# An order of its own for ScalarE during attention: sigmoids, roundings and weight conversions in source order

## The chip, the core and the metric

The kernel runs on one core of a Trainium2 chip. TensorE (PE, with its weight loads as PEld), VectorE (DVE), ScalarE (ACT), GpSimd (POOL) and SyncE (SP) work side by side and are held together by semaphores. The metric is the device time of one execution in microseconds (us). Three executions of the kernel before took 722.46 to 725.92 us, with a median of 723.36 us.

## The reference

The computation is a chain of three layers, all in float32.

```python
scores = scale * q @ k.T - log(S)            # batch 4, 12 heads, S = 448, head_dim 64
x = (1 / (1 + exp(-scores))) @ v             # sigmoid attention, -> (1792, 768)
h = max(x @ w1, x @ w2, x @ w3) @ w_out      # max of three products
h = h @ w_in                                 # (1792, 1024)
solu = h * softmax(h); ln = layernorm(solu) * g_ln
out = ln @ w_out2                            # (1792, 768)
```

The weights arrive as 64-bit floats (their two 32-bit words are in the input), so the core makes float32 values of them itself.

## The kernel before

**Precision.** A large product is computed as three TensorE products of rounded parts: every operand is split into a rounded high part (`copy`, L48) and the rest (`rest`, L54), and high times high, high times low and low times high are added in PSUM.

**Attention** (the loop from L317) goes over 24 pairs of heads, `pr` from 0 to 23. For each pair, `prep_qk` (L222) splits k and q on VectorE into `kt` and `qt`; `scores(pr, c)` (L266), for four chunks c of 128 rows (448 rows and 64 of padding), issues six matmuls into a PSUM tile `sc` and one sigmoid on ScalarE (L281) that writes `sf`. There are three `sc` tiles, so the fourth chunk of a pair waits until the pair's first sigmoid has emptied its tile. `attend(pr, c)` (L286) multiplies `sf` by v into a PSUM tile `av`. After a pair's fourth chunk, ScalarE rounds `av` to `xh` (L50 by way of L303) and VectorE writes the rest `xl` (L55 by way of L304). In each turn TensorE does the four scores of pair pr, the last two `attend` of pair pr - 1, and the first two `attend` of pair pr. k and q are loaded two pairs ahead by SyncE's DMA queue into two buffers, v into three.

**Weights.** In the background runs a queue of generators. `prepare(key)` (L163) turns one 128 x 768 piece of weights into float32 and splits it: a scaling on ScalarE (L147, out `y_...`, called a conversion here), then on VectorE a shift (L150), a shift with OR (L153), a rounding (L52) and a rest (L55). The 64-bit words of a piece (768 KB) lie in one of two buffers `raw`. Once L153 has read one, `load_next` (L132) issues the load of the next piece from GpSimd's DMA queue. Each `run_bg(n)` in the source takes n steps of the queue; a piece has five steps (scaling, shift, shift with OR, rounding, rest). The eleven pieces of `first` (L114: eight of `wi`, three of `wo`) are the ones that are queued during attention.

**After attention** `gen_w` (L242) multiplies w_out by w_in once (tiles `pw`), and then follow the products with the three weights (`pg`, L356) and with the combined weights (`h`, L428), the layer norm, and the last product (`po`, L503).

**What sets the order.** The source is traced into instructions, and a scheduler puts each engine's instructions into a fixed order by readiness and priorities of its own. Each engine then executes its row strictly from first to last. L68 exempts TensorE: `tc.manual_schedule` keeps its instructions in the order of the source. ScalarE, VectorE and the DMA queues are ordered by the scheduler; it may pull an instruction ahead of others that stand earlier in the source.

Of the kernel before, what the change touches and what calls it, by code (L numbers as in the profile page):

```python
# [33 lines left out]
def sigmoid_attention_max_moe_solu_ln(tc, q, k, v, w123, wo, wi, w2, g, out):  # L34
# [13 lines left out]
    def copy(eng, dst, src):  # L48
        if eng is act:
            act.copy(dst, src)  # L50
        else:
            eng.tensor_copy(dst, src)  # L52

    def rest(eng, dst, src, hi):  # L54
        eng.tensor_tensor(out=dst, in0=src, in1=hi.bitcast(F32), op=ALU.subtract)  # L55
# [8 lines left out]
    def shut(*cms):  # L64
        for cm in cms:
            cm.__exit__(None, None, None)
# [30 lines left out]
    def run_bg(n=1):  # L97
        while n > 0 and bg:
            if next(bg[0], "end") == "end":
                bg.popleft()  # L100
            else:
                n -= 1
# [29 lines left out]
    def load_next():  # L132
        i = state["load"]
        if i >= len(stream):
            return
        state["load"] += 1
        key = stream[i]
        t = rawp.tile([P, U, 2], I32, tag="raw", name=f"raw{i}", bufs=RAWS)
        pool.dma_start(out=t, in_=source(key).rearrange("p (n t) -> p n t", t=2))
        raws[key] = t  # L140
# [74 lines left out]
    def load_v(pr):  # L215
        if pr >= NP:
            return
        vr = apool.tile([P, 2, 4, D], F32, tag="vr", name=f"vr{pr}", bufs=3)
        sp.dma_start(out=vr, in_=v[pr])
        v_ops[pr] = vr  # L220

    def prep_qk(pr):  # L222
        if pr >= NP:
            return
        qr, kr = qk_raw.pop(pr)
        kt = apool.tile([P, 2, SX], F32R, tag="kt", name=f"kt{pr}")
        qt = apool.tile([P, 2, S], F32R, tag="qt", name=f"qt{pr}")
        qk_ops[pr] = (qt, kt)
        copy(dve, kt[:, 0], kr)
        copy(dve, qt[:, 0], qr)  # L230
        rest(dve, kt[:, 1], kr, kt[:, 0])
        rest(dve, qt[:, 1], qr, qt[:, 0])
        load_qk(pr + 2)
# [32 lines left out]
    def scores(pr, c):  # L266
        qt, kt = qk_ops[pr]
        sc = ps_sc.tile([P, 2, 512], F32, tag="sc", name=f"sc{pr}_{c}")
        terms = ((0, 0), (0, 1), (1, 0))
        for t, (x, y) in enumerate(terms):  # L270
            for j in range(2):
                rows = slice(j * D, (j + 1) * D)
                pe.matmul(  # L273
                    sc[:, j, :S],
                    lhsT=kt[rows, x, c * P : (c + 1) * P],
                    rhs=qt[rows, y],
                    start=(t == 0),
                    stop=(t == len(terms) - 1),
                )
        sf = apool.tile([P, 2, S], F32, tag="sf", name=f"sf{pr}_{c}", bufs=6)  # L280
        act.activation(sf, sc[:, :, :S], AF.Sigmoid, bias=bias_s, scale=1.0 / math.sqrt(D))  # L281
        weights[(pr, c)] = sf
# [3 lines left out]
    def attend(pr, c):  # L286

        b, hp = divmod(pr, NPAIR)
        vr = v_ops[pr]
        if c == 0:  # L290
            pas[pr] = ps_av.tile([P, 512], F32, tag="av", name=f"av{pr}")
        pa = pas[pr]
        sf = weights.pop((pr, c))
        for j in range(2):
            pe.matmul(pa[j * D : (j + 1) * D, :S], lhsT=vr[:, j, c], rhs=sf[:, j], start=(c == 0), stop=(c == 3))  # L295
        if c < 3:
            return
        pas.pop(pr)
        v_ops.pop(pr)
        if hp == 0:  # L300
            xs_hi[b] = xps[b].tile([P, KC, S], F32R, name=f"xh{b}")
            xs_lo[b] = xps[b].tile([P, KC, S], F32R, name=f"xl{b}")
        copy(act, xs_hi[b][:, hp], pa[:, :S])  # L303
        rest(dve, xs_lo[b][:, hp], pa[:, :S], xs_hi[b][:, hp])  # L304
        load_v(pr + 3)


    act.preload_act_table_set("sigmoid_and_others")
    for pr in range(2):
        load_qk(pr)  # L310
# [6 lines left out]
    for pr in range(NP):  # L317
        if pr == 1:
            load_next()
            load_next()  # L320
        for c in range(4):
            scores(pr, c)
            if c == 1:
                prep_qk(pr + 1)
        if pr > 1:
            run_bg(1)
        if pr > 0:
            attend(pr - 1, 2)
            attend(pr - 1, 3)
        if pr > 1:  # L330
            run_bg(1)
        attend(pr, 0)
        attend(pr, 1)
        if pr > 1:
            run_bg(1)
    attend(NP - 1, 2)
    attend(NP - 1, 3)
    run_bg(1 << 20)
    for cm, _ in reversed(ps1):
        shut(cm)  # L340
# [245 lines left out]
```

## Time and profile before

| | |
|---|---|
| median of three executions | 723.36 us (722.46 to 725.92) |
| the profiled execution | 724.43 us, of which the span is 722.7 us |
| PE busy | 698.5 us (97%) |
| DVE busy | 334.0 us (46%) |
| ACT busy | 237.7 us (33%) |
| chain that ended last | PE 93%, DMA 3% |

The span runs from the first to the last instruction of the profile; 1.73 us of the execution lie around it. A busy PE isn't PE at its peak, since matmuls overlap; so the pace of attention is read from the distance between the starts of one pair and the next. The granted clock is 1.00 at TensorE's full 2.4 GHz and 0.50 at 1.2 GHz; values between are means over a stretch in which it changed.

### The profile page before, as it was taken

How to read it: one execution, taken by the hardware profiler on the slowest of the kernel's cores; microseconds unless marked ns; L12 is line 12 of the kernel's file. 1: busy time of each engine (PE TensorE's matmuls, PEld its weight loads, DVE VectorE, ACT ScalarE, POOL GpSimd, SP SyncE). 2: the span in 40 equal slices, each digit the busy share in tenths (PEclk: the TensorE clock that was granted, in tenths of full speed). 3: DMA queues.
4: the chain of work that ended last, by engine and by line, in shares of the span. 5: the costliest groups of instructions: out<-in, count | busy, mean ns of one | idle time of the engine just before them, and what ended most of it. 6: DMA issues, size and time to landing. Idle time of an engine off the chain costs nothing.

```text
span 722.7 us, 9080 instructions
## 1 busy us (share of the span) xinstructions
PE 698.5 (97%) x3664; PEld 576.0 (80%) x3664; DVE 334.0 (46%) x610; ACT 237.7 (33%) x396; POOL 32.6 (5%) x59
## 2 busy tenths in 40 slices
PE   6777999999999999999999999999999999999997
PEld 3334555556888999999999999988999999999997
DVE  4897444431552354435433322215755555555440
ACT  5576666663222033132310200202322332322221
POOL 1111000000221000000000000000000000000000
PEclk9899999999999999999999999999999999999999
DMA  7777544420564124232331000800322222222221
GB/s 261 264 259 258 170 127 126 127 72 13 203 221 175 44 88 132 92 127 88 111 107 44 1 0 1 349 0 1 110 93 97 81 81 80 81 81 81 89 94 44
DMA packets 29707, 80.82 MB, mean 112 GB/s; under 512 B 3424, under 2 KB 12896, under 8 KB 28896
## 3 DMA queue, kind: packets, MB, share of 16 engines
q1 hardware_dynamic: 22176, 42.48, 17.1%
q0 software_dynamic: 7488, 37.75, 15.0%
q8 instruction: 29, 0.48, 0.3%
q14 instruction: 14, 0.11, 0.1%
HBM read 62.13 MB, written 18.09 MB: 111 GB/s over the span
## 4 chain that ended last, share of the span: by engine, by line
PE 93%; DMA 3%; DVE 1%; issue 1%; ACT 1%; SPq 0%; ACTq 0%
PE pg L239 36%; PE po L512 16%; PE h L436 16%; PE av L295 10%; PE sc L273 8%; PE pw L239 7%; DMA kr<-in_k 1%; ACT sf L281 1%; DMA raw<-in_wo 1%; DMA raw<-in_wi 1%; DVE y_wi L153 0%; PE pt L496 0%; DVE qt L55 0%; DVE y_wi L150 0%; DVE kt L55 0%
## 5 line engine op out<-in xcount | busy, mean ns | idle before, releaser
L239 PE MATMUL pg<-xh,r_w 128*128 128x448 f32 x864 | 245.5, 365 | 0.0
L239 PEld LDWEIGHTS pg<-xh,r_w 128*128 128x128 f32 x864 | 162.3, 188 | 12.9
L239 PE MATMUL pg<-xl,r_w 128*128 128x448 f32 x432 | 157.8, 365 | 0.0
L436 PE MATMUL h<-wf,hh 128*128 128x512 f32 x336 | 103.8, 390 | 0.8 <-issue 0.8
L281 ACT ACTIVATE sf<-sc,bias_s 128x896 f32<-128x896 f32 x96 | 88.9, 1006 | 31.4 <-PE sc L273 31.4
L273 PE MATMUL sc<-qt,kt 64*128 64x448 f32 x576 | 73.8, 392 | 19.7 <-ACT sf L281 14.4
L273 PEld LDWEIGHTS sc<-qt,kt 64*128 64x128 f32 x576 | 52.4, 191 | 47.9 <-ACT sf L281 22.9
L239 PEld LDWEIGHTS pg<-xl,r_w 128*128 128x128 f32 x432 | 81.1, 188 | 6.4
L295 PE MATMUL av<-sf,vr 128*64 128x448 f32 x384 | 82.4, 574 | 0.0
L374 DVE TENSOR_TENSOR h<-pg,h 128x448 f32<-128x448 f32 x48 | 29.9, 623 | 101.9 <-PE pg L239 101.9
L512 PE MATMUL po<-w2h,lh 128*128 128x384 f32 x224 | 75.0, 335 | 0.0
L512 PE MATMUL po<-w2h,ll 128*128 128x384 f32 x224 | 75.0, 335 | 0.0
L512 PE MATMUL po<-w2l,lh 128*128 128x384 f32 x224 | 74.9, 334 | 0.0
L436 PEld LDWEIGHTS h<-wf,hh 128*128 128x128 f32 x336 | 62.8, 188 | 13.6 <-issue 1.1
L436 PE MATMUL h<-wf,hl 128*128 128x512 f32 x168 | 65.6, 390 | 0.0
L295 PEld LDWEIGHTS av<-sf,vr 128*64 128x64 f32 x384 | 26.8, 144 | 44.8 <-issue 38.3
L448 DVE TENSOR_REDUCE st<-h 128x1 f32<-128x1024 f32 x14 | 17.1, 1222 | 84.9 <-PE h L436 84.9
L147 ACT ACTIVATE y_w<-raw 128x768 f32<-128x768 f32 x26 | 23.3, 897 | 100.3 <-DVE r_w L55 93.2
L50 ACT CAST hh<-h 128x128 fp32r<-128x128 f32 x84 | 18.1, 295 | 93.3 <-PE h L436 86.5
L239 PE MATMUL pw<-wih,r_wo 128*128 128x512 f32 x144 | 44.6, 390 | 0.0
L372 ACT COPY h<-pg 128x448 f32<-128x448 f32 x24 | 12.8, 533 | 92.3 <-PE pg L239 92.3
L512 PEld LDWEIGHTS po<-w2h,lh 128*128 128x128 f32 x224 | 42.1, 188 | 0.5
(68 smaller groups left out, 626.1 us busy)
## 6 DMA issues: line engine op xcount, KB each, us to landing
raw<-in_w POOLq DMA_DIRECT2D x26, 768.0 KB, 4.6
kr<-in_k SPq DMA_DIRECT2D x24, 256.0 KB, 2.8
raw<-in_wi POOLq DMA_DIRECT2D x8, 768.0 KB, 4.8
vr<-in_v SPq DMA_DIRECT2D x24, 256.0 KB, 3.7
w_d<-ws POOLq DMA_DIRECT2D x12, 512.0 KB, 3.7
wf<-w_d SPq DMA_DIRECT2D x6, 1024.0 KB, 9.9
u_d<-ub SPq DMA_DIRECT2D x12, 512.0 KB, 2.9
ut<-u_d SPq DMA_DIRECT2D x48, 128.0 KB, 3.1
```

What stands on the lines that cost most here:

```text
L50: act.copy(dst, src)
L147: act.activation(y, raw.bitcast(F32)[:, :, 1], AF.Prelu, scale=2.0**-112, alpha=2.0**32)
L239: pe.matmul(ps, lhsT=l, rhs=r, start=(i == 0), stop=(i == n - 1))
L273: pe.matmul(sc[:, j, :S], lhsT=kt[rows, x, c * P : (c + 1) * P], rhs=qt[rows, y], start=(t == 0), stop=(t == len(terms) - 1),)
L281: act.activation(sf, sc[:, :, :S], AF.Sigmoid, bias=bias_s, scale=1.0 / math.sqrt(D))
L295: pe.matmul(pa[j * D : (j + 1) * D, :S], lhsT=vr[:, j, c], rhs=sf[:, j], start=(c == 0), stop=(c == 3))
L372: act.copy(hv, ps[:, :S])
L374: dve.tensor_tensor(out=hv, in0=ps[:, :S], in1=hv, op=ALU.max)
L436: pe.matmul(ps[:, n], lhsT=l, rhs=r, start=(f == 0 and i == 0), stop=(f == FC - 1 and i == 2))
L448: dve.tensor_reduce(out=nmax, in_=ps, axis=AX.XY, op=ALU.max, negate=True)
L512: pe.matmul(ps[:, :hw], lhsT=l, rhs=r, start=(kc == 0 and i == 0), stop=(kc == K2 - 1 and i == 2))
```

## The change

The source of the attention loop gets a second `manual_schedule`, for ScalarE, from the table load to the end of the loop. Within it ScalarE issues in source order. The three `run_bg(1)` of a pair, which stood between the scores and the `attend` calls from pair 2 on, become one `run_bg(3)` at the end of the turn, from pair 3 on. Three steps of five mean that at most one scaling falls into a turn. VectorE, GpSimd and SyncE are ordered by the scheduler as before.

```diff
+    first_order = tc.manual_schedule(engines={mybir.EngineType.Activation})
+    first_order.__enter__()
     act.preload_act_table_set("sigmoid_and_others")
...
             scores(pr, c)
             if c == 1:
                 prep_qk(pr + 1)
-        if pr > 1:
-            run_bg(1)
         if pr > 0:
             attend(pr - 1, 2)
             attend(pr - 1, 3)
-        if pr > 1:
-            run_bg(1)
         attend(pr, 0)
         attend(pr, 1)
-        if pr > 1:
-            run_bg(1)
+        if pr > 2:
+            run_bg(3)
     attend(NP - 1, 2)
     attend(NP - 1, 3)
+    shut(first_order)
     run_bg(1 << 20)
```

TensorE's and GpSimd's instructions stand in the same order before and after. ScalarE's row at the start of attention, before (`sf1_2` is the sigmoid of pair 1, chunk 2; `y_wi_0_1` the scaling of the second piece of `wi`; the last number of a name is a serial number):

```order
L147 ACTIVATE y_wi_0_0_304<-raw0_193 128x768
L281 ACTIVATE sf0_0_149<-sc0_0_142,bias_s_94 128x896
L281 ACTIVATE sf0_1_158<-sc0_1_151,bias_s_94 128x896
L281 ACTIVATE sf0_2_177<-sc0_2_170,bias_s_94 128x896
L281 ACTIVATE sf0_3_186<-sc0_3_179,bias_s_94 128x896
L281 ACTIVATE sf1_0_204<-sc1_0_197,bias_s_94 128x896
L147 ACTIVATE y_wi_0_1_386<-raw1_195 128x768
L281 ACTIVATE sf1_1_213<-sc1_1_206,bias_s_94 128x896
L281 ACTIVATE sf1_2_232<-sc1_2_225,bias_s_94 128x896
L147 ACTIVATE y_wi_0_2_507<-raw2_367 128x768
L281 ACTIVATE sf1_3_241<-sc1_3_234,bias_s_94 128x896
```

The same place after the change:

```order
L281 ACTIVATE sf0_0_151<-sc0_0_144,bias_s_94 128x896
L281 ACTIVATE sf0_1_160<-sc0_1_153,bias_s_94 128x896
L281 ACTIVATE sf0_2_179<-sc0_2_172,bias_s_94 128x896
L281 ACTIVATE sf0_3_188<-sc0_3_181,bias_s_94 128x896
L281 ACTIVATE sf1_0_206<-sc1_0_199,bias_s_94 128x896
L281 ACTIVATE sf1_1_215<-sc1_1_208,bias_s_94 128x896
L281 ACTIVATE sf1_2_234<-sc1_2_227,bias_s_94 128x896
L281 ACTIVATE sf1_3_243<-sc1_3_236,bias_s_94 128x896
L50 CAST xh0_249<-av0_190 128x448
```

The scalings have left the first three pairs. The eleven of `first` stand now one by one behind the `xh` of pairs 2, 3, 5, 7, 8, 10, 12, 13, 15, 17 and 18; before, all were ahead of pair 7's sigmoids, as were two more pieces of `wo`. Those two, `wo_3` and `wo_4`, which the source has after attention and which the scheduler still pulls ahead, are the exception to one per turn. ScalarE's row around them after the change:

```order
L147 ACTIVATE y_wi_1_3_1349<-raw9_1158 128x768
L281 ACTIVATE sf19_0_1360<-sc19_0_1353,bias_s_94 128x896
L281 ACTIVATE sf19_1_1369<-sc19_1_1362,bias_s_94 128x896
L281 ACTIVATE sf19_2_1388<-sc19_2_1381,bias_s_94 128x896
L281 ACTIVATE sf19_3_1397<-sc19_3_1390,bias_s_94 128x896
L50 CAST xh3_1403<-av18_1344 128x448
L147 ACTIVATE y_wo_2_1418<-raw10_1284 128x768
L147 ACTIVATE y_wo_3_1729<-raw11_1414 128x768
L281 ACTIVATE sf20_0_1427<-sc20_0_1420,bias_s_94 128x896
...
L147 ACTIVATE y_wo_4_1763<-raw12_1481 128x768
L50 CAST xh3_1403<-av19_1409 128x448
L281 ACTIVATE sf21_0_1492<-sc21_0_1485,bias_s_94 128x896
```

Before, the same stretch held sigmoids and `xh` alone. On VectorE the splitting of pair 1 stood in this order, with a shift of the first weight piece in it:

```order
L52 CAST kt1_160<-kr1_123 128x512
L150 TENSOR_SCALAR y_wi_0_0_304<-y_wi_0_0_304 128x768
L52 CAST qt1_161<-qr1_124 128x448
L55 TENSOR_TENSOR kt1_160<-kr1_123,kt1_160 128x512
L55 TENSOR_TENSOR qt1_161<-qr1_124,qt1_161 128x448
```

After the change it stands as that of pair 0 does:

```order
L52 CAST kt1_162<-kr1_125 128x512
L55 TENSOR_TENSOR kt1_162<-kr1_125,kt1_162 128x512
L52 CAST qt1_163<-qr1_126 128x448
L55 TENSOR_TENSOR qt1_163<-qr1_126,qt1_163 128x448
```

From the first tile of `gen_w` on, every engine's instructions stand in the same order before and after.

## Rows read from the trace of the kernel before

**Rows 1.** Windows: stretch, length, busy PE, PEld, DVE, ACT, POOL, clock, DMA share, GB/s.

```profile
0.00:69.14 69.14, 49.43 (x273) 24.80 (x273) 51.60 (x88) 40.34 (x48) 9.95 (x21) 0.90 0.75 258
69.14:172.56 103.42, 103.42 (x690) 54.40 (x688) 40.51 (x80) 71.13 (x86) 0.54 (x1) 1.00 0.37 118
172.56:722.70 550.14, 545.68 (x2706) 496.80 (x2704) 241.94 (x443) 126.21 (x263) 22.08 (x37) 1.00 0.26 92
```

**Rows 2.** Timeline, TensorE: start, length, what, count [idle before, who ended it].

```profile
10.57 0.88 PE L273 MATMUL sc<-qt,kt 64*128 64x448 f32 x6 [1.60 <-ACT sf L281]
...
13.91 2.65 PE L273 MATMUL sc<-qt,kt 64*128 64x448 f32 x22 [0.41 <-DVE qt L55]
16.50 3.23 PE L295 MATMUL av<-sf,vr 128*64 128x448 f32 x16
19.66 1.49 PE L273 MATMUL sc<-qt,kt 64*128 64x448 f32 x12
...
26.69 1.49 PE L273 MATMUL sc<-qt,kt 64*128 64x448 f32 x6 [4.14 <-ACT sf L281]
28.11 5.56 PE L295 MATMUL av<-sf,vr 128*64 128x448 f32 x16
...
69.14 2.94 PE L273 MATMUL sc<-qt,kt 64*128 64x448 f32 x24
...
165.07 2.91 PE L273 MATMUL sc<-qt,kt 64*128 64x448 f32 x24
...
172.56 0.50 PE L239 MATMUL pw<-wih,r_wo 128*128 128x512 f32 x1
```

**Rows 3.** Timeline, ScalarE, the first pairs and two neighbours of the steady stretch.

```profile
8.73 0.89 ACT L147 ACTIVATE y_wi<-raw 128x768 f32<-128x768 f32 x1 [6.71 <-DMA raw<-in_wi]
9.52 3.69 ACT L281 ACTIVATE sf<-sc,bias_s 128x896 f32<-128x896 f32 x4
...
24.86 0.89 ACT L147 ACTIVATE y_wi<-raw 128x768 f32<-128x768 f32 x1 [2.82 <-DVE y_wi L153]
25.64 3.69 ACT L281 ACTIVATE sf<-sc,bias_s 128x896 f32<-128x896 f32 x4
...
106.11 3.70 ACT L281 ACTIVATE sf<-sc,bias_s 128x896 f32<-128x896 f32 x4 [1.83 <-PE sc L273]
109.74 0.53 ACT L50 CAST xh<-av 128x448 fp32r<-128x448 f32 x1
```

**Rows 4.** Timeline, VectorE, the splitting of pairs 0 and 1.

```profile
3.44 0.43 DVE L52 CAST kt<-kr 128x512 fp32r<-128x512 f32 x1 [3.44 <-DMA kr<-in_k]
4.93 0.63 DVE L55 TENSOR_TENSOR qt<-qr,qt 128x448 fp32r<-128x448 f32 x1
11.53 0.43 DVE L52 CAST kt<-kr 128x512 fp32r<-128x512 f32 x1 [5.97 <-DMA kr<-in_k]
13.24 0.62 DVE L55 TENSOR_TENSOR qt<-qr,qt 128x448 fp32r<-128x448 f32 x1
```

**Rows 5.** Timeline, one raw buffer: last read, reload issued, scaling of what it loaded.

```profile
61.99 0.96 DVE L153 SCALAR_TENSOR_TENSOR y_wo<-raw,y_wo 128x768 int32<-128x768 int32 x1
63.60 0.53 POOL L139 DMA_DIRECT2D raw<-in_wo  x1 [7.24 <-ACT sf L281]
68.15 0.92 ACT L147 ACTIVATE y_wo<-raw 128x768 f32<-128x768 f32 x1 [1.89 <-DMA raw<-in_wo]
```

**Rows 6.** Source view of L139, all forty raw loads.

```profile
DMA to landing us min/median/max: 4.3/4.7/9.0
```

**Rows 7.** The page: GB/s in 40 slices, and two kinds of load with their size.

```profile
GB/s 261 264 259 258 170 127 126 127 72 13 203 221 175 44 88 132 92 127 88 111 107 44 1 0 1 349 0 1 110 93 97 81 81 80 81 81 81 89 94 44
kr<-in_k SPq DMA_DIRECT2D x24, 256.0 KB, 2.8
raw<-in_wi POOLq DMA_DIRECT2D x8, 768.0 KB, 4.8
```

## Prediction

> **What bounds the kernel now.** I read the windows first. The span falls into three stretches [rows 1]. From 0 to 69.14 us TensorE is busy for 49.43 us, at a mean clock of 0.90. From 69.14 us to 172.56 us, and from there to the end, it is busy nearly all the time at a clock of 1.00. The reader should see that all the slack of TensorE is in the first tenth of the span, while ScalarE is not full there either: 40.34 of 69.14 us. So something is waiting for something, and no engine has too much work.
>
> Second, the timeline of TensorE gives the pace [rows 2]. Pair 7 starts its scores at 69.14 and pair 23 at 165.07, so 16 pairs take 95.93 us, 5.996 us each, without a gap. Pair 2 starts at 19.66, so the five pairs 2 to 6 take 49.48 us, where the steady pace would give 29.98. The waits in that stretch end with a sigmoid (the 4.14 us ahead of 26.69), and behind that wait TensorE is slow for a while: sixteen `av` matmuls take 5.56 us where they took 3.23 at 16.50, and six score matmuls 1.49 us where they took 0.88.
>
> Third, ScalarE's timeline says why the sigmoids were late [rows 3]. At 8.73 it starts a weight scaling for which it has waited 6.71 us (a transfer), and only then, at 9.52, the first four sigmoids. At 24.86 it starts another scaling, 2.82 us late, since VectorE hadn't yet freed what it needs; pair 2's sigmoids follow at 25.64, and the wait of TensorE at 26.69 ends on them. ScalarE takes its row strictly in turn, so a scaling that is not ready holds back sigmoids that are. The thirteen scalings that stand among the first seven pairs are what bounds the stretch.
>
> **The change part by part.** *Scalings out of the first pairs.* The first three pairs lose all of theirs. What is then late next? Pair 1 cannot start before its k has landed: VectorE's split begins at 11.53 after a wait of 5.97 us for a DMA [rows 4]. The same loads are issued as before, so I keep 11.53. In pair 0 the same four instructions, in the order that pair 1 now gets, start the q rest 1.49 us after the first cast (4.93 - 3.44). Pair 1's q rest thus starts at 13.02 instead of 13.24: 0.22 us gained, and TensorE, which resumes at 13.91 on that rest [rows 2], resumes at 13.69. Its row then runs through as before (16.50 to 19.66 has no wait in it), and pair 2 starts at 19.44 instead of 19.66. The idle 1.60 us ahead of 10.57 goes from there, but TensorE then waits those 1.6 us for pair 1, so nothing else is gained.
>
> *Pairs 2 to 6 at the steady pace.* With no weight scaling before its sigmoids, pair 2 is in the state of the pairs from 7 on: four sigmoids, `xh`, then 1.83 us in which ScalarE waits for the scores [rows 3]. These five pairs gain 49.48 - 29.98 = 19.50 us. This already holds the time that TensorE lost at the lower clock level. With the 0.22, the sum is 19.7 us.
>
> *Scalings into the steady pairs.* Eleven turns get one scaling. It takes 0.89 us, and the next instruction starts 0.79 us after it (8.73 to 9.52, 24.86 to 25.64) [rows 3]. It stands behind `xh`, in the 1.83 us, of which 1.04 us stay. Cost nothing; the cover is TensorE's first chunk of the next pair. Without this cover each would cost 0.79 us. On VectorE a piece costs about 2.8 us: in the first stretch it is busy for 51.60 us with thirteen pieces less a few instructions and eight splits, and in the second 40.51 us for 16 pairs, 2.5 each, so (51.60 - 8 x 2.5) / 11.5. A turn with a piece then holds 5.3 of 6.0 us. It fits, and kt and qt are made a whole turn ahead, so a late one costs nothing at first.
>
> *Loads.* A scaling waits for its 768 KB. A buffer is free once L153 has read it, and the data are ready for ScalarE 1.61 + 4.55 = 6.16 us after that instruction starts (61.99, 63.60, 68.15) [rows 5]. Call the start of a turn's sigmoids S. `xh` starts at S + 3.63 [rows 3], the scaling at about S + 4.1, L153 at S + 5.6, and the new piece is ready at S + 11.8. For the eleven pieces of `first` the same buffer is wanted three or four turns later (18 us or more), so they never wait. `wo_3` and `wo_4` do: `wo_3` needs the buffer of the piece scaled one turn earlier, at S + 10.9, and waits 0.9 us; the next sigmoid, due at S + 12.0, comes at 12.6. `wo_4` needs the buffer of the turn just gone; it starts at S + 11.8, `xh` follows at 12.6, and the next sigmoid starts at 13.1 instead of 12.0. Both delays are measured against the same clock of turns, so the second, 1.1 us, contains the first. TensorE's fourth chunk waits for that first sigmoid (26.69 follows 25.64 by the 1.0 us of one), so I charge it in full. The bounds are 0 and, with the slowest landing of the trace (9.0 against 4.55) [rows 6], 5.5 us. I take 1.1, since the row at 63.60 is such a reload with a piece behind it.
>
> *After attention* nothing moves: `gen_w` wants the last pieces of `first` three turns (18 us) after they are done. The 550.14 us from 172.56 on stay.
>
> *The sum.* 19.7 - 1.1 = 18.6 us. The profiled execution took 724.43 us with a span of 722.70; it becomes 704.1 and 705.8. It was 1.07 us above the median of 723.36, from which the same sum gives 704.8. I say 705.3.
>
> What the rows cannot exclude at the start is a clock that falls in the idle time ahead of pair 1. The 1.60 us ahead of 10.57 did not slow the six matmuls behind it (0.88 us), the 4.14 us did, for (1.49 - 0.88) + (5.56 - 3.23) = 2.9 us [rows 2]. So 0 to 2.9; I take 0.
>
> **The rivals.** *The reloads are slow.* The raw loads are issued by GpSimd, and the slowest took 9.0 us to land, twice the median of 4.7 [rows 6]; in the stretch where the new turns lie VectorE will be busier than it was. With 9.0 `wo_4` costs 5.5 us instead of 1.1: 709.7. Against it: the reload at 63.60 took 4.55 with VectorE at three quarters. (The Trainium skill, "SBUF — State Buffer", section on SBUF's two separate sides, says that a DMA issued from GpSimd has its descriptors written over a port that VectorE's float32 copies between SBUF tiles lock, so that it seems blocked by them. By it the landings would grow with VectorE's casts; the median of 4.7 us bears out little of it.)
>
> *The scalings do not hide.* If the 1.83 us are not free, because `xh` comes later or the scores earlier in a denser turn, all thirteen cost 0.79 us: 10.3 us, so 715.6. For it: ScalarE becomes the second tightest engine. Against it: the 1.83 us were measured behind the same four sigmoids and the same `xh`, at the same pace [rows 3].
>
> *The transfers bound the turns: slower.* A steady turn loads k and v (256 KB each) and q (224 KB by its shape), and now three fifths of 768 KB: 1197 KB or 1.226 MB in 6.0 us, 204 GB/s [rows 7]. Before, the steady stretch moved 118 GB/s [rows 1]. If the loads got only 170 GB/s, as in the fifth slice, a turn would take 7.2 us, and the seventeen turns from 3 to 19 would lose 20.5 us: 725.8. It decides from 173 GB/s downward, where the gain is used up (18.6 / 17 = 1.1 us a turn). Against it: the first four slices moved 258 to 264 GB/s with the same kinds of load [rows 7].
>
> *The order isn't kept.* If sigmoids still waited for scalings nothing would change: 723.4. The new row of ScalarE, as shown, speaks against it.
>
> **How the numbers follow.** The forecast has 0.74, the slow reloads 0.11, the scalings that don't hide 0.09, the transfers 0.04, no change 0.02. The forecast's own range goes from 702.6 (the fastest run, 722.46, less 19.7 and a little) to 708.2 (with the clock). Up to the slow reloads and a little of a late start, the range is 702 to 711; what lies above holds 0.15. About 0.5% (3.6 us) is what a measurement of this kernel can tell from no change. Forecast, slow reloads and scalings that don't hide are faster: 0.94. No change: 0.02. The transfers: 0.04 slower.
>
> **What would show it.** The scores of pair 2 start at 19.4 us and those of pair 23 at about 146.5, with 6.0 us between neighbours; `pw` starts at 154.0. ScalarE's first sigmoid starts before 8 us, its 1.83 us shrink to about 1.0 in eleven turns. TensorE waits for a sigmoid once or twice, in turns 20 and 21, for 1 us. The prediction is wrong if turns with a scaling are longer than those without, if k is waited for after pair 1, or if `gen_w` waits for weights.

## The result and the profile after

The changed kernel takes 706.51 us (median of four executions, 705.0 to 708.48) against 724.5 us (four executions, 722.46 to 725.92; a fourth has moved the median from the 723.36 us that the prediction started from). The ratio is 0.9755, with a 95% interval of 0.9716 to 0.9795: faster by 2.5%. The forecast was 705.3 us in a range of 702 to 711. The profiled execution was the slowest of the four: it took 708.48 us with a span of 706.7 us, so its span is 16.0 us shorter than before, where the sum had 18.6.

The windows of the changed kernel, cut where pair 2 starts and where `gen_w` starts (columns as in [rows 1]):

```profile
0.00:21.35 21.35, 13.65 (x73) 8.00 (x73) 8.54 (x17) 9.45 (x10) 1.89 (x9) 0.92 0.70 240
21.35:156.51 135.16, 133.47 (x890) 70.02 (x888) 86.03 (x150) 102.24 (x123) 7.35 (x13) 1.00 0.56 185
156.51:706.70 550.19, 545.70 (x2706) 496.83 (x2704) 241.83 (x443) 126.18 (x263) 22.07 (x37) 1.00 0.26 92
```

What comes after attention takes 550.19 us, as before (550.14 in [rows 1]). TensorE's slack is now in the first 21 us, with 1.7 us more in the 135 us behind them. In that long middle the clock is 1.00, and the DMA engines move 185 GB/s instead of 118, since the weight pieces are spread over it.

TensorE's timeline (columns as in [rows 2]):

```profile
5.18 4.38 PE L273 MATMUL sc<-qt,kt 64*128 64x448 f32 x24 [5.18 <-DVE qt L52]
9.49 1.72 PE L295 MATMUL av<-sf,vr 128*64 128x448 f32 x8
13.64 4.11 PE L273 MATMUL sc<-qt,kt 64*128 64x448 f32 x24 [2.42 <-DVE qt L52]
17.68 3.74 PE L295 MATMUL av<-sf,vr 128*64 128x448 f32 x16
21.35 2.92 PE L273 MATMUL sc<-qt,kt 64*128 64x448 f32 x24
...
129.24 2.09 PE L273 MATMUL sc<-qt,kt 64*128 64x448 f32 x18
132.08 0.87 PE L273 MATMUL sc<-qt,kt 64*128 64x448 f32 x6 [0.75 <-ACT sf L281]
...
139.06 0.87 PE L273 MATMUL sc<-qt,kt 64*128 64x448 f32 x6 [0.94 <-ACT sf L281]
...
156.51 0.50 PE L239 MATMUL pw<-wih,r_wo 128*128 128x512 f32 x1
```

Pair 2 starts at 21.35 and pair 20 at 129.24: 18 turns in 107.89 us, 5.994 us each, eleven of them with a scaling. Only two waits for a sigmoid are left, in turns 20 and 21. The 4.14 us of [rows 2] and the others like it are gone.

ScalarE, a turn with a scaling, and the place where `wo_2`, `wo_3` and `wo_4` are scaled:

```profile
32.39 0.93 ACT L147 ACTIVATE y_wi<-raw 128x768 f32<-128x768 f32 x1
34.32 3.70 ACT L281 ACTIVATE sf<-sc,bias_s 128x896 f32<-128x896 f32 x4 [1.00 <-PE sc L273]
...
128.28 0.93 ACT L147 ACTIVATE y_wo<-raw 128x768 f32<-128x768 f32 x1
130.23 0.90 ACT L147 ACTIVATE y_wo<-raw 128x768 f32<-128x768 f32 x1 [1.02 <-DMA raw<-in_wo]
131.03 3.69 ACT L281 ACTIVATE sf<-sc,bias_s 128x896 f32<-128x896 f32 x4
136.78 0.91 ACT L147 ACTIVATE y_wo<-raw 128x768 f32<-128x768 f32 x1 [2.06 <-DMA raw<-in_wo]
137.59 0.52 ACT L50 CAST xh<-av 128x448 fp32r<-128x448 f32 x1
138.00 3.71 ACT L281 ACTIVATE sf<-sc,bias_s 128x896 f32<-128x896 f32 x4
```

The 1.83 us of [rows 3] have become 1.00, and the sigmoids still end their wait on the scores, not on the scaling. Around `wo_3` and `wo_4` it is the other way: ScalarE waits 1.02 and 2.06 us for a load, and sigmoids follow late.

### The profile page after: what moved, and what is told of

It reads as the page before. It is cut to its first block, busy times and chain, and to the rows that moved or that the text cites. A ratio compares the mean times of both kernels' runs of the same rounds, so it can differ in the third digit from the quotient of the medians.

```text
span 706.7 us, 9079 instructions
## 1 busy us (share of the span) xinstructions
PE 692.8 (98%) x3664; PEld 574.8 (81%) x3664; DVE 336.4 (48%) x610; ACT 237.9 (34%) x396; POOL 31.3 (4%) x59
## 4 chain that ended last, share of the span: by engine, by line
PE 97%; DMA 1%; ACT 0%; DVE 0%; issue 0%; SPq 0%; ACTq 0%
PE pg L239 37%; PE po L511 17%; PE h L435 16%; PE av L295 11%; PE sc L273 9%; PE pw L239 7%; DMA kr<-in_k 1%; PE pt L495 0%; ACT sf L281 0%; DVE kt L55 0%; DVE qt L55 0%; ACT xh L50 0%; ACT ob L512 0%; DVE kt L52 0%; SPq L219 0%
## 5 line engine op out<-in xcount | busy, mean ns | idle before, releaser
L281 ACT ACTIVATE sf<-sc,bias_s 128x896 f32<-128x896 f32 x96 | 89.0, 1006 | 37.5 <-PE sc L273 37.4
L273 PEld LDWEIGHTS sc<-qt,kt 64*128 64x128 f32 x576 | 52.4, 191 | 36.5 <-issue 18.7
L273 PE MATMUL sc<-qt,kt 64*128 64x448 f32 x576 | 72.5, 389 | 9.4 <-DVE qt L52 7.6
L295 PE MATMUL av<-sf,vr 128*64 128x448 f32 x384 | 78.0, 548 | 0.0
L295 PEld LDWEIGHTS av<-sf,vr 128*64 128x64 f32 x384 | 25.6, 138 | 41.3 <-issue 33.1
```

Source lines behind the costliest of these rows:

```text
L273: pe.matmul(sc[:, j, :S], lhsT=kt[rows, x, c * P : (c + 1) * P], rhs=qt[rows, y], start=(t == 0), stop=(t == len(terms) - 1),)
```

## The experiments

Each run was compared with executions of the kernel before on the same chip. The edits are against the changed kernel, except that of the first run, which is against the kernel before.

**ScalarE's order alone.** The two lines of the manual order, with the background steps where they were.

```diff
+    first_order = tc.manual_schedule(engines={mybir.EngineType.Activation})
+    first_order.__enter__()
     act.preload_act_table_set("sigmoid_and_others")
...
     attend(NP - 1, 3)
+    shut(first_order)
     run_bg(1 << 20)
```

> The first part alone: ScalarE in source order during attention, with the three single background steps of a pair where they were before, from pair 2 on. The rate stays three steps a turn, so the scalings are as thinly spread as in the changed kernel; they stand behind the fourth sigmoid or behind xh, and their weights landed turns ago. My theory (sigmoids were late because scalings that weren't ready stood ahead of them): the whole gain is here, 705 to 709 us, pairs 6.0 us apart from pair 2 on. Rival (the new place of the background steps, behind all attend calls, makes the gain): 715 us or more.

Measured: 706.57 us, ratio 0.975 (0.9717 to 0.9783). The whole gain is here. From pair 2 (21.45) to pair 9 (63.43) the turns take 6.00 us each.

**The steps alone.** One `run_bg(3)` at the end of a turn from pair 3 on; ScalarE is ordered by the scheduler.

```diff
-    first_order = tc.manual_schedule(engines={mybir.EngineType.Activation})
-    first_order.__enter__()
...
-    shut(first_order)
```

> The second part alone: three background steps at the end of a turn from pair 3 on, and the scheduler orders ScalarE as before. It pulls the scalings to the front again: thirteen stand ahead of pair 7's sigmoids, in nearly the same places as before the change. My theory: as before the change, 720 to 727 us. Rival (the place of the steps matters): 705 to 715 us.

Measured: 724.37 us, ratio 0.9997 (0.9977 to 1.0017). TensorE's timeline shows the waits of the kernel before again:

```profile
28.14 1.49 PE L273 MATMUL sc<-qt,kt 64*128 64x448 f32 x6 [3.53 <-ACT sf L281]
29.55 5.42 PE L295 MATMUL av<-sf,vr 128*64 128x448 f32 x16
```

These two answer to 26.69 and 28.11 in [rows 2]. Where the steps stand in the source made no difference here as long as the scheduler could pull the scalings ahead.

**Two scalings a turn.** This separates the order from the rate: source order is kept, but the weights are wanted sooner.

```diff
         if pr > 2:
-            run_bg(3)
+            run_bg(10)
```

> The changed kernel with ten background steps a turn instead of three, so two scalings a turn from turn 3 to 8, ScalarE still in source order. Two scalings take 1.6 us and would fit in the 1.83 us if their weights were there. My theory (what delays sigmoids is waiting for a weight piece that is not ready, since a buffer is read and reloaded in about 7.7 us): the two buffers are wanted again one turn later, the second is ready at about S + 14 and the sigmoids due at S + 12, so each of these turns takes 9 to 10 us instead of 6.0, and the time is 716 to 730 us, though the order is the source's. Rival (the order alone makes the gain, the rate does not matter): 705 to 708 us.

Measured: 722.85 us, ratio 0.9975 (0.9947 to 1.0003). The gain is gone, and with it the rival. At the end of turn 4 two scalings stand behind `xh`, each waits for its load, and pair 5's sigmoids wait behind them (ScalarE's timeline, then TensorE's):

```profile
36.12 0.53 ACT L50 CAST xh<-av 128x448 fp32r<-128x448 f32 x1
38.21 0.91 ACT L147 ACTIVATE y_wi<-raw 128x768 f32<-128x768 f32 x1 [1.56 <-DMA raw<-in_wi]
42.19 0.89 ACT L147 ACTIVATE y_wi<-raw 128x768 f32<-128x768 f32 x1 [3.07 <-DMA raw<-in_wi]
42.98 3.68 ACT L281 ACTIVATE sf<-sc,bias_s 128x896 f32<-128x896 f32 x4
```

```profile
37.50 2.09 PE L273 MATMUL sc<-qt,kt 64*128 64x448 f32 x18
44.03 1.49 PE L273 MATMUL sc<-qt,kt 64*128 64x448 f32 x6 [4.43 <-ACT sf L281]
45.45 4.90 PE L295 MATMUL av<-sf,vr 128*64 128x448 f32 x16
50.27 2.12 PE L273 MATMUL sc<-qt,kt 64*128 64x448 f32 x18
```

Turn 5 takes 12.77 us (37.50 to 50.27), the next four from 6.3 to 11.9 us. The two scalings of turn 3, whose loads had been issued at 1.32 and 2.31 us, fitted: the turn that follows takes 6.0 us (31.50 to 37.50). What costs is a piece that isn't there.

**Scalings doubled and tripled.** The eleven pieces are scaled two or three times into the same tile. The edit for two is shown; for three, its `1` is a `2`.

```diff
-        for op in to_f32(raw, y):
+        ops = to_f32(raw, y)
+        for _ in range(1 if key in first else 0):
+            ops[0]()
+        for op in ops:
```

> The changed kernel with the scaling of each of the eleven first pieces issued twice (the second writes the same values). My theory (a scaling lies in the 1.83 us in which ScalarE waits for the next scores; 1.00 us are left in the trace of the changed kernel): another 0.79 us still fits, the turns stay 6.0 us; only the reloads of wo_3 and wo_4 come 0.8 us later. 706 to 708.5 us. Rival (scalings are paid for): 0.79 us in eleven turns, 715 us.

> The same with three scalings each. My theory: 3 x 0.79 = 2.37 us do not fit in 1.83 us, so the first sigmoid of eleven turns comes about 0.55 us late and TensorE's fourth chunk with it: 6 us, and the reloads of wo_3 and wo_4 come 1.6 us later; 711 to 715 us. Rival (there is slack behind the fourth chunk as well): 706 to 709 us.

Measured: 709.59 us (706.7 to 710.46) with two, a ratio of 0.9807 (0.9781 to 0.9834); 717.38 us with three, 0.9926 (0.9908 to 0.9944). Both are above the range that my theory gave, and the turns say why. With two, ScalarE has no idle time left, yet the turns are as short as before (ScalarE's timeline, then TensorE's; L276, L284 and L298 are L273, L281 and L295 here):

```profile
32.80 1.86 ACT L147 ACTIVATE y_wi<-raw 128x768 f32<-128x768 f32 x2
34.68 3.70 ACT L284 ACTIVATE sf<-sc,bias_s 128x896 f32<-128x896 f32 x4
```

```profile
33.76 2.85 PE L276 MATMUL sc<-qt,kt 64*128 64x448 f32 x24
36.54 3.23 PE L298 MATMUL av<-sf,vr 128*64 128x448 f32 x16
39.70 2.85 PE L276 MATMUL sc<-qt,kt 64*128 64x448 f32 x24
...
133.42 0.89 PE L276 MATMUL sc<-qt,kt 64*128 64x448 f32 x6 [2.53 <-ACT sf L284]
134.24 4.85 PE L298 MATMUL av<-sf,vr 128*64 128x448 f32 x16
```

So the cover is as I said: the turn from 33.76 to 39.70 takes 5.94 us. The loss is at one place, in the turn of `wo_3` and `wo_4`: one wait of 2.53 us instead of 0.75 and 0.94, and then sixteen `av` matmuls that take 4.85 us instead of 3.23. With three, each of ten turns waits about 0.7 us (I had 0.55, from a spacing of 0.79 us; scalings of one tile follow each other at 0.93), and the last waits 3.54 us. TensorE's timeline, this last wait:

```profile
140.36 0.96 PE L276 MATMUL sc<-qt,kt 64*128 64x448 f32 x6 [3.54 <-ACT sf L284]
```

**The first two weight pieces later.** In the changed kernel they are loaded from 1.3 us on, while k and q of pair 1 are on their way, and not read before turn 3.

```diff
-        pool.dma_start(out=t, in_=source(key).rearrange("p (n t) -> p n t", t=2))
+        (sp if i < 2 else pool).dma_start(out=t, in_=source(key).rearrange("p (n t) -> p n t", t=2))
```

> The changed kernel, but the first two weight pieces (768 KB each, not read before turn 3) are loaded by SyncE's queue behind the loads of k, q and v of the first four pairs, instead of at 1.3 us by GpSimd's. My theory on the 1.9 us by which pair 2 started later than I predicted (k of pair 1 landed at 12.0 us behind 1.5 MB of weights, TensorE idled 2.4 us and then ran pair 1 slowly): k lands by 8 or 9 us, TensorE runs pair 1 right behind pair 0 at full speed, pair 2 starts at 17 to 18 us instead of 21.35, and the time is 702 to 704 us. Rival (k is late by its own queue, not by the weights): no change, 706 to 707 us.

Measured: 704.36 us (703.44 to 704.87), ratio 0.9719 (0.9689 to 0.975). That is 0.4 us above my range, and the mechanism is shown. VectorE starts pair 1's split at 6.25 us instead of 12.04 (the changed kernel's line first), and TensorE goes from pair 0 to pair 1 without a wait:

```profile
12.04 0.43 DVE L52 CAST kt<-kr 128x512 fp32r<-128x512 f32 x1 [6.25 <-DMA kr<-in_k]
```

```profile
6.25 0.43 DVE L52 CAST kt<-kr 128x512 fp32r<-128x512 f32 x1 [0.68 <-DMA kr<-in_k]
```

```profile
4.97 5.13 PE L273 MATMUL sc<-qt,kt 64*128 64x448 f32 x24 [4.97 <-DVE qt L52]
10.03 2.33 PE L295 MATMUL av<-sf,vr 128*64 128x448 f32 x8
12.29 2.86 PE L273 MATMUL sc<-qt,kt 64*128 64x448 f32 x24
15.08 3.23 PE L295 MATMUL av<-sf,vr 128*64 128x448 f32 x16
18.23 2.90 PE L273 MATMUL sc<-qt,kt 64*128 64x448 f32 x24
```

Pair 2 starts 3.1 us sooner than in the changed kernel. I had expected 17 to 18 us; pair 0's own matmuls are slower than I allowed for (5.13 us for 24).

**ScalarE in source order to the end of `gen_w`.**

```diff
     attend(NP - 1, 3)
-    shut(first_order)
     run_bg(1 << 20)
...
+    shut(first_order)
     shut(ws_cm, wi_cm)
```

> The changed kernel, with ScalarE in source order up to the end of gen_w, so that the scalings of wo_3 and wo_4 stand in gen_w and not in turns 19 and 20. My theory (the waits of TensorE of 0.75 and 0.94 us in turns 20 and 21 come from these two scalings): both waits go, pw starts 1.7 us earlier; if gen_w then does not wait for wo_3, 704 to 706 us. Rival (gen_w, which wants wo_3 at its seventh tile, waits for the reload chain that now starts later): the 1.7 us come back in gen_w, 706 to 710 us.

Measured: 704.9 us (704.4 to 705.11), ratio 0.9729 (0.9694 to 0.9765). `wo_3` is now scaled behind the third tile of `gen_w` (ScalarE's timeline):

```profile
165.09 0.59 ACT L50 CAST ws<-pw 128x512 fp32r<-128x512 f32 x1 [3.49 <-PE pw L239]
165.57 0.90 ACT L147 ACTIVATE y_wo<-raw 128x768 f32<-128x768 f32 x1
```

No wait of TensorE for a sigmoid is left, turns 20 and 21 take 6.0 us like the others (127.02, 133.01, 139.01), and `gen_w` waits for nothing; from `pw` at 152.50 to the end it takes 550.1 us:

```profile
127.02 2.91 PE L273 MATMUL sc<-qt,kt 64*128 64x448 f32 x24
...
133.01 2.91 PE L273 MATMUL sc<-qt,kt 64*128 64x448 f32 x24
...
139.01 2.91 PE L273 MATMUL sc<-qt,kt 64*128 64x448 f32 x24
```

Of the 4.0 us by which `pw` starts sooner than in the changed kernel's profile, 2.2 are not the edit's: pair 2 starts at 19.14 instead of 21.35, with the same loads issued. In that execution k of pair 1 landed 1.1 us sooner, TensorE waited 0.85 us for pair 1 instead of 2.42, and pair 1's matmuls were faster (24 scores in 3.22 us instead of 4.11). The remaining 1.8 us are, within 0.1, the two waits (0.75 + 0.94).

**Both together.**

> The changed kernel with both edits of the earlier runs: the first two weight pieces loaded behind k, q and v, and ScalarE in source order to the end of gen_w. My theory (the late start and the two waits of wo_3 and wo_4 are separate and add up): pair 2 starts at about 18.2 us, no wait for a sigmoid, pw at about 151.7 us, 702 to 704 us. Rival (they overlap): as the better of the two, 704 to 705 us.

Measured: 702.35 us (702.15 to 703.34), ratio 0.9717 (0.9701 to 0.9732). TensorE's timeline:

```profile
18.23 2.91 PE L273 MATMUL sc<-qt,kt 64*128 64x448 f32 x24
...
144.09 2.91 PE L273 MATMUL sc<-qt,kt 64*128 64x448 f32 x24
146.93 4.73 PE L295 MATMUL av<-sf,vr 128*64 128x448 f32 x24
151.59 0.50 PE L239 MATMUL pw<-wih,r_wo 128*128 128x512 f32 x1
```

From 18.23 to 144.09 there are 21 turns of 5.993 us, without a wait, and `pw` starts 4.9 us sooner than in the changed kernel's profile, where the start (3.1 us) and the two waits (1.69 us) make 4.8: the two effects add up. All its executions are below the fastest of the changed kernel (705.0); the intervals of the two ratios still touch (0.9732 against 0.9716).

## Why the prediction was right

**What bounds the first stretch.** Right: the scalings that stand among the first sigmoids and wait for their pieces. Three runs show it together. Source order alone brings the whole gain, the place of the steps none of it, and source order with two scalings a turn loses it again. Of the rival that the order isn't kept nothing is left.

**Pairs 2 to 6 at the steady pace.** Right: 5.994 us a turn from pair 2 on, where the 5.996 of [rows 2] were taken.

**Pair 1 and the start.** The step "the first three pairs lose all of theirs" had pair 2 at 19.44; it started at 21.35. I kept 11.53 us for the landing of k; it was 12.04. That alone moved little: TensorE started pair 1 at 13.64 with nothing of it done, where I had it resume at 13.69 with two matmuls done, a loss of 0.2 us. The other 1.7 us are slow matmuls: the 1.60 us of idle time ahead of 10.57 in [rows 2] became 2.42 us in one piece ahead of pair 1, after which 24 score matmuls took 4.11 us instead of 2.91 and sixteen `av` 3.74 instead of 3.23. I had bounded this at 0 to 2.9 us and taken 0, so this term of the sum was mis-sized. It is 1.9 us of the 2.6 by which the profiled execution missed the sum.

Nor is it a fixed cost. Six kernels have the same start up to pair 2, and in their traces pair 2 starts at 19.14 (order up to `gen_w`), 19.52 (two scalings a turn), 19.80 (scalings tripled), 21.35 (the changed kernel), 21.45 (order alone) and 21.75 us (scalings doubled). In the first three pair 1's scores took 3.22 or 3.23 us, in the others 4.11 to 4.64. Taking 0 was about right for half of them, so that the median came as near to the forecast as 1.2 us is partly luck.

One sign that I had named did show: VectorE waited 0.39 us for k after pair 1, at 14.54 for pair 2's. TensorE did not wait for it.

**The scalings in the steady turns.** Right: nothing is paid, 1.00 us of the 1.83 is left where I had 1.04. The run with two scalings a piece uses up even that without a longer turn, the one with three pays for it. The rival of scalings that do not hide falls. On VectorE a piece costs 3.04 us (0.56 + 0.96 + 0.56 + 0.96 in the turn at 123.25) where I had 2.8; it still fits.

**The reloads of `wo_3` and `wo_4`.** The mechanism was right, and its place: turns 20 and 21, no others. The size was 1.69 us (0.75 + 0.94) instead of 1.1. The way from L153's start to the scaling took 6.94 us (129.84 to 136.78) where I had 6.16 from [rows 5]:

```profile
129.84 0.96 DVE L153 SCALAR_TENSOR_TENSOR y_wo<-raw,y_wo 128x768 int32<-128x768 int32 x1
131.46 0.85 POOL L139 DMA_DIRECT2D raw<-in_wo  x1 [5.46 <-ACT y_wo L147]
```

The slow landings did not come at this place, and the rival had them from another one: the 9.0 us of [rows 6] is the second load of all, issued at 2.31 us while the first loads of k, q and v were under way. The raw loads issued between 40 and 180 us landed in 4.5 to 6.1 us before the change and in 4.5 to 6.8 after it. That the second delay contains the first held as well: the sigmoids of turn 20 came 0.8 us late and those of turn 21 1.8.

**The transfers.** The middle stretch moves 185 GB/s at a share of 0.56, and kt and qt are never late there.

**The sum**, with what was measured: 18.6 - 1.9 - 0.6 = 16.1 us, against 16.0 in the profiled execution. The two medians differ by 18.0 us.

## What to carry to other kernels

An engine that takes its row strictly in turn should not have an instruction that waits for a load ahead of one that TensorE waits for, however short it is; the place for it is the idle time that the engine has in every turn, at a rate that the reload of its buffer can follow. A scheduler that may reorder can undo such a placement in the source, as it did here. What is loaded early but read late should be queued behind what the first matmuls need.

## What the runs showed of the hardware

The first pair's matmuls are slow although the rows of the clock say 1.00: 24 score matmuls took 5.13 us, against 2.86 for the next 24 scores, which follow without a wait of TensorE, in a stretch (0 to 12.29 us of the run with late weight pieces) whose granted clock is 1.00. How soon they get faster differs: 4.38 us in the changed kernel.

Slow matmuls after idle time were seen again: after 2.42 us the mean granted clock from 13.64 to 21.35 us is 0.78, between the two levels (1.2 and 2.4 GHz); after 2.53 us the sixteen `av` matmuls took 4.85 us. The waits of 0.75 and 0.94 us left the next sixteen at 3.23 us. But the length of the idle time alone does not tell which it will be. In the run with the scalings doubled 1.62 us were enough ahead of pair 1: its 24 scores took 4.64 us at a mean granted clock of 0.63. In the run of the steps alone 2.37 us did nothing, and the clock stayed at 1.00 behind them (the first line is from the doubled scalings, the others from the steps alone):

```profile
14.03 4.64 PE L276 MATMUL sc<-qt,kt 64*128 64x448 f32 x24 [1.62 <-DVE qt L52]
```

```profile
45.92 0.87 PE L273 MATMUL sc<-qt,kt 64*128 64x448 f32 x6 [2.37 <-ACT sf L281]
46.72 3.23 PE L295 MATMUL av<-sf,vr 128*64 128x448 f32 x16
```

The landing of k of pair 1, behind the same loads, came between 10.97 and 12.59 us in the traces of eight kernels that issue them alike. Whether these loads also widen the spread of the times is not shown: over four executions it is 1.4 and 1.2 us in the two kernels that have them out of the way, and between 0.7 and 3.8 us in five that have not.

With two scalings a piece, the sixteen turns from 33.76 to 128.80 took 5.94 us each instead of 5.99, those without a scaling too. What shortens them stays open.
